# A retention block and a squared-ReLU feed-forward in one kernel: the fifth piece of w_in is converted behind chunk 4's mask, and one half step of the first layer moves ahead of chunk 4's scores

## The chip, the cores and the metric

The kernel runs on one core of a Trainium2 chip. The metric is the time of one execution on the device in microseconds; the median of several executions is given. The trace of one further execution shows what each engine did and when.

## The reference

Two blocks follow one another. The first is retention without a softmax: with `rel[i,j] = i - j`, every head has its own decay, and the masked, decayed scores are multiplied by `v`. The second is a feed-forward with a squared ReLU. q, k, v are float32; the two weights come as float64 and are rounded to float32 inside the kernel.

```python
# retention: batch 8, heads 8, seq 576, head_dim 64
scores = scale * np.matmul(q, k.transpose(0, 1, 3, 2))
gamma = 1.0 - 2.0 ** (-5.0 - np.arange(H, dtype=np.float32))
Dmat = np.where(rel >= 0, gamma[:, None, None] ** rel[None, :, :], 0.0)
attn = np.matmul(scores * Dmat[None], v)
# bridge: (B,H,S,D) -> (B*S, H*D), 4608 tokens x 512
x = np.ascontiguousarray(attn.transpose(0, 2, 1, 3)).reshape(B * S, H * D)
# feed-forward: w_in 512 x 2048, w_out 2048 x 512
h = np.maximum(x @ w_in, 0.0)
out = h * h @ w_out
```

## The kernel before

Retention goes over 40 chunks of up to 128 tokens (five per sequence: four of 128 and one of 64; chunk 4 is the short one). 512 tokens (chunks 0 to 3) make a block of the feed-forward. Everything that this change touches happens in the first tenth of the run, where retention, the first block of the first layer, and the conversion of w_in from float64 are woven together by the order in which the program issues them. Engines run on their own, but each one takes its instructions in the order issued.

**Conversion.** w_in is cut into 16 pieces. A piece is fetched raw (`fetch_w`, 512 KB) and rounded by six steps: five for VectorE (DVE), and one, `beside`, of two instructions for ScalarE (ACT). The generator `w_in_parts` yields the steps; `convert(n)` issues the next n. Pieces 0 to 3 take 6 steps each; piece 4 takes 8, as the first two of piece 5 come inside it; after that every piece j is `beside j, one j+1, two j+1, three j, four j, last j`.

```python
def round_parts(j):
    ...
    def one():      # exponent bits
        nc.vector.tensor_scalar(exp, hi, 20, 0x7FF, op0=ALU.logical_shift_right, op1=ALU.bitwise_and)
    def two():
        nc.vector.tensor_scalar(bits, as_dst(j, hi), 0xFFFFF, 0x100000, op0=ALU.bitwise_and, op1=ALU.bitwise_or)
    def beside():
        nc.scalar.activation(exp, exp, AF.Relu, bias=exp_bias[:, 0:1], scale=2.0 ** 23)
        nc.scalar.activation(frac, lo, AF.Copy, scale=2.0 ** -52)
    def three():
        nc.vector.scalar_tensor_tensor(t, bits, 2.0 ** -20, as_dst(j, frac), op0=ALU.mult, op1=ALU.add)
    def four():
        nc.vector.tensor_tensor(t, t, as_dst(j, exp_of(j)), op=ALU.mult)
    def five():
        nc.vector.scalar_tensor_tensor(bits, as_dst(j, hi), 0x80000000, bits, op0=ALU.bitwise_and, op1=ALU.bitwise_or)

def w_in_parts():
    parts = [round_parts(j) for j in range(N_W1)] + [[None] * 2]
    for j in range(N_W1):                       # N_W1 = 16
        one, two, beside, three, four, five = parts[j]
        if j <= N_ALONE:                        # N_ALONE = 4
            yield from (one, two)
        yield beside
        if j >= N_ALONE:
            yield from parts[j + 1][0:2]
        yield three
        yield four
        def last(five=five):
            five()
            n_made[0] += 1
            if n_next[0]:
                fetch_raw(2)
        yield last
```

**A step of the first block.** `first_in(j)` multiplies piece j with the block's tokens; `first_in(j, (0,))` and `(1,)` do only one half of the tokens. `step()` takes the next from the list: second halves of pieces 0, 1, 2, then pieces 3 to 15 whole.

```python
def first_in(j, halves=(0, 1)):
    assert n_made[0] > j
    ...
    p = ps_f.tile([128, 2, HT], F32, tag="f", name="h_ps")
    for c in range(N_DM):
        nc.tensor.matmul(p..., lhsT=w[:, c, :], rhs=xT[0][:, c, lo * HT:hi * HT], ...)
    nc.scalar.activation(t, p, AF.Relu)
    some(2)                                     # what is queued, the squares of steps before among it
    queue.append(lambda: nc.vector.tensor_tensor(t, t, t, op=ALU.mult))
    ...
```

**A chunk.** `turn(i)` transposes k and q (TensorE, PE), ACT copies kT, DVE makes qT (times the decay from chunk 4 on); `scores(i)` multiplies them and DVE masks the result. From chunk 4 on, the transposes and the scores take turns in one PSUM buffer. `retain_a/b/c(i)` make chunk i's output; `retain_b` ends with a small ACT copy (u_sb from x_ps), and `retain_c` writes more into x_ps.

```python
def turn(i):
    p = ps_t.tile([128, 2, 512], F32, tag="t", name="t_ps")...      # bufs=1
    ... nc.tensor.transpose(...)
    nc.scalar.copy(to, p[...])                                      # kT
    nc.vector.tensor_tensor(to, p[...], dq[...], op=ALU.mult)       # qT, i >= N_EARLY
def scores(i):
    both = ps_t.tile([128, 2, 512], F32, tag="t", name="sc_ps")...  # i >= N_EARLY
    ... nc.tensor.matmul(sc..., lhsT=kT..., rhs=qT...)
    nc.vector.tensor_tensor(r[:cs], both[:cs], msk..., op=ALU.mult) # ret
    nc.gpsimd.tensor_tensor(vs[:cs], ...)
```

**The order in the main loop** (N_EARLY = 4):

```python
for i in range(N_CH + 1):
    if i <= N_EARLY:
        if i == 1: convert(2)
        elif i == 2: convert(5)
        if i >= 1:
            retain_a(i - 1)
            if i < 3: warm(4, False)
            elif i == N_EARLY: turn(i)
            else:
                convert(1); first_in(1, (0,)); convert(5)
            retain_b(i - 1)
            ...
            retain_c(i - 1)
        convert((0, 1, 1, 0, 0)[i])
        scores(i)
        if i == 2:
            convert(5); first_in(0, (0,))
        elif i == 3:
            convert(1); first_in(2, (0,)); convert(5)
        elif i == N_EARLY:
            fetch_raw(2)
            convert(1)
            for _ in range(2):
                step(); convert(5); convert(1)
        if i < N_EARLY: ... turn(i + 1)
    else:
        retain_a(i - 1)
        if i < N_CH: turn(i)
        ffn(i - 1, 0)          # first block: convert(6), step()
        retain_b(i - 1)
        if i < N_CH: scores(i)
        retain_c(i - 1)
        ffn(i - 1, 1)          # first block: step(), convert(6), step(), convert(6)
    if i == 0: fetch_raw(2)
    if i + 3 < N_CH: load(i + 3)
    if 0 < i < N_EARLY: fetch_raw(1)
```

After the first block the first layer runs on with seven products in place of eight (Strassen-Winograd, `ffn_in`), and then the second layer (`inner`, `outer`); neither is touched.

Of the kernel before, what the change touches and what calls it, by code (L numbers as in the profile page):

```python
# [40 lines left out]
def kernel(  # L41
# [87 lines left out]
    N_EARLY = TOK // C  # L129
# [65 lines left out]
    def fetch_w(j):  # L195
        if j < len(pieces) and wide:
            nc.sync.dma_start(raw_of(j).bitcast(I64).rearrange("p (c f) -> p c f", c=N_DM), piece_src(j))
# [38 lines left out]
    def sum_w_in(mp):  # L236

        a11, a12, a21, a22, s1, s2, s4 = (w_in[mp][:, :, j, :, :].rearrange("p m c f -> p m (c f)") for j in range(NP))
        return [lambda: nc.vector.tensor_tensor(s1, a21, a22, op=ALU.add),
                lambda: nc.vector.tensor_tensor(s2, s1, a11, op=ALU.subtract),  # L240
                lambda: nc.vector.tensor_tensor(s4, a12, s2, op=ALU.subtract),
                lambda: nc.vector.tensor_tensor(a21, a11, a21, op=ALU.subtract)]
# [43 lines left out]
    def fetch_raw(count):  # L286

        for _ in range(count):
            if n_raw[0] < min(N_W1, n_made[0] + N_RAW):
                fetch_w(n_raw[0])  # L290
                n_raw[0] += 1
# [25 lines left out]
    def convert(count):  # L317
        for _ in range(count):
            f = next(w_in_steps, None)
            f and f()  # L320
# [39 lines left out]
    def rows(half, n=64):  # L360
        return slice(64 * half, 64 * half + n)
# [13 lines left out]
    def scale_q(i, engine):  # L375

        ci, t = chunks[i][1], loaded[i][0]
        engine.tensor_tensor(t, t, dv[:, :, NCH + ci:NCH + ci + 1].to_broadcast([C, H, D]), op=ALU.mult)
# [22 lines left out]
    def scores(i):  # L401

        b_, ci, c0, cs = chunks[i]
        qT, kT = st[i]["qT"], st[i]["kT"]
        if i < N_EARLY:

            sc = [ps_f.tile([128, 512], F32, tag="f", name="sc_ps")[:, 0:256].rearrange("p (h t) -> p h t", h=HP) for e in range(2)]
        else:
            both = ps_t.tile([128, 2, 512], F32, tag="t", name="sc_ps")[:, :, 0:256].rearrange("p e (h t) -> p e h t", h=HP)
            sc = [both[:, e, :, :] for e in range(2)]  # L410
        n_h = cs // CH
        for hp in range(HP):
            for h in range(n_h):
                for e in range(2):
                    t = slice(CH * h, CH * h + CH)
                    nc.tensor.matmul(sc[e][rows(h), hp, :], lhsT=kT[rows(e), hp, t], rhs=qT[rows(e), hp, t],  # L416
                                     start=True, stop=True, skip_group_check=True)
        r = st[i]["ret"] = work2.tile([128, 2, HP, CH], F32, tag="ret", name="ret")
        if i < N_EARLY:
            for e in range(2):  # L420
                nc.vector.tensor_tensor(r[:cs, e, :, :], sc[e][:cs], msk[:cs, 0, :, :].to_broadcast([cs, HP, CH]), op=ALU.mult)
        else:
            nc.vector.tensor_tensor(r[:cs], both[:cs], msk[:cs].to_broadcast([cs, 2, HP, CH]), op=ALU.mult)
        vs = st[i]["vs"] = loaded[i][2]
        nc.gpsimd.tensor_tensor(vs[:cs], vs[:cs],  # L425
                                dv[:cs, :, ci:ci + 1].to_broadcast([cs, H, D]), op=ALU.mult)
# [21 lines left out]
    def retain_a(i):  # L448

        b_, ci, c0, cs = chunks[i]  # L450
        xp[0] = ps_x.tile([128, 2, 256], F32, tag="x", name="x_ps", padded_shape=[128, 2, 512])
        clean.clear()
        if ci == 0:
            u_ps[0] = ps_u.tile([128, HP, D], F32, tag="u", name="u_ps")
        if cs < C:
            return
        own, grow = within(i, 1)
        for j in range(0, len(own), 2):
            for f in own[j:j + 2] + grow[j:j + 2]:
                f()  # L460
        grown(i, 0)
# [51 lines left out]
    def sum_x(n):  # L513

        x = xT[n]
        b11, b12 = x[:, 0:2, 0:HT], x[:, 0:2, HT:]
        b21, b22 = x[:, 2:4, 0:HT], x[:, 2:4, HT:]
        t1, t2, t4 = (xs_room[:, j, :, :] for j in range(3))
        xs[n] = {"B11": b11, "T3": b12, "B21": b21, "B22": b22, "T1": t1, "T2": t2, "T4": t4}
        return [lambda: nc.vector.tensor_tensor(t1, b12, b11, op=ALU.subtract),  # L520
                lambda: nc.vector.tensor_tensor(t2, b22, t1, op=ALU.subtract),  # L521
                lambda: nc.vector.tensor_tensor(b12, b22, b12, op=ALU.subtract),
                lambda: nc.vector.tensor_tensor(t4, b21, t2, op=ALU.subtract)]
# [21 lines left out]
    def some(count=1):  # L545
        for f in queue[:count]:
            f and f()
        del queue[:count]

    def first_in(j, halves=(0, 1)):  # L550

        assert n_made[0] > j
        wi, m, e = pieces[j]
        mp, mm = divmod(m, 2)
        p = ps_f.tile([128, 2, HT], F32, tag="f", name="h_ps")
        w = w_in[mp][:, mm, 2 * e:2 * e + 2, :, :].rearrange("p s c f -> p (s c) f")
        lo, hi = halves[0], halves[-1] + 1
        p = p[:, lo:hi, :]
        for c in range(N_DM):
            nc.tensor.matmul(p.rearrange("p h t -> p (h t)"), lhsT=w[:, c, :], rhs=xT[0][:, c, lo * HT:hi * HT],  # L560
                             start=(c == 0), stop=(c == N_DM - 1))

        t = g_room[mp % 2][:, 3:7:3, mm, :] if e else g_room[mp % 2][:, 0:5:4, mm, :]
        t = t[:, lo:hi, :]
        nc.scalar.activation(t, p, AF.Relu)

        some(2)
        queue.append(lambda: nc.vector.tensor_tensor(t, t, t, op=ALU.mult))
        if mm and e and hi == 2:
            queue.append(lambda: [nc.sync.dma_start(  # L570
                g_dram[0, a:b, :, 2 * mp:2 * mp + 2, :].rearrange("s p m t -> p s (m t)"),
                g_room[mp % 2][:, a:b, :, :].rearrange("p s m t -> p s (m t)")) for a, b in QUARTERS])
        if j >= N_W1 - 4:

            sums_w.setdefault(0, sum_w_in(0)).pop(0)()
            if n_next[0] > 1:
                if 1 not in sums_x:
                    sums_x[1] = sum_x(1)
                sums_x[1].pop(0)()
# [80 lines left out]
    def step():  # L660
        n, f, *args = steps.pop(0)
        done[0] += 1
        f(*args)
# [54 lines left out]
    for i in range(N_CH + 1):  # L718
        if i <= N_EARLY:

            if i == 1:
                convert(2)
            elif i == 2:
                convert(5)
            if i >= 1:
                retain_a(i - 1)
                if i < 3:
                    warm(4, False)
                elif i == N_EARLY:
                    turn(i)  # L730
                else:
                    convert(1)
                    first_in(1, (0,))
                    convert(5)
                retain_b(i - 1)
                if i < 3:
                    warm(4, False)
                retain_c(i - 1)
            convert((0, 1, 1, 0, 0)[i])
            scores(i)  # L740
            if i == 2:
                convert(5)
                first_in(0, (0,))
            elif i == 3:
                convert(1)
                first_in(2, (0,))
                convert(5)
            elif i == N_EARLY:
                fetch_raw(2)
                convert(1)  # L750
                for _ in range(2):
                    step()
                    convert(5)
                    convert(1)
            if i < N_EARLY:
                if i + 1 < N_EARLY:
                    scale_q(i + 1, nc.gpsimd)
                if i < 2:
                    warm(6, False)
                if i + 1 < N_EARLY:  # L760
                    turn(i + 1)
        else:
            if i == N_EARLY + 1:
                gone[0] = TOK
            retain_a(i - 1)
            if i < N_CH:
                turn(i)
            ffn(i - 1, 0)
            retain_b(i - 1)
            if i < N_CH:  # L770
                scores(i)
            retain_c(i - 1)
            ffn(i - 1, 1)
        if i == 0:
            fetch_raw(2)
        if i + 3 < N_CH:
            load(i + 3)
        if 0 < i < N_EARLY:
            fetch_raw(1)
# [239 lines left out]
```

## Time and profile before

| what | value |
|---|---|
| time, median of 3 (lowest to highest) | 999.09 us (998.42 to 999.68) |
| span of the profiled execution | 996.4 us |
| PE, busy | 975.9 us, 98% of the span |
| DVE, busy | 747.7 us, 75% |
| ACT, busy | 190.7 us, 19% |
| GpSimd (POOL), busy | 83.9 us, 8% |

The profile's second part cuts the span into 40 slices of 24.9 us and gives each engine's busy share in tenths, and PEclk, the clock granted to PE in tenths of the full one:

```
PE   7789999999999999999999999999999999999998
DVE  4687497657878797897886777877777677777765
PEclk9889999999999999999999999999999999999999
DMA  9993565754786879779558999674674757556351
```

Apart from the last slice, only the first three have PE below nine tenths. That is where chunks 0 to 5 and the start of the first block lie.

In the DMA row, 9 means that the 16 DMA engines were at work nearly all of the slice.

### The profile page before, as it was taken

How to read it: one execution, taken by the hardware profiler on the slowest of the kernel's cores; microseconds unless marked ns; L12 is line 12 of the kernel's file. 1: busy time of each engine (PE TensorE's matmuls, PEld its weight loads, DVE VectorE, ACT ScalarE, POOL GpSimd, SP SyncE). 2: the span in 40 equal slices, each digit the busy share in tenths (PEclk: the TensorE clock that was granted, in tenths of full speed). 3: DMA queues.
4: the chain of work that ended last, by engine and by line, in shares of the span. 5: the costliest groups of instructions: out<-in, count | busy, mean ns of one | idle time of the engine just before them, and what ended most of it. 6: DMA issues, size and time to landing. Idle time of an engine off the chain costs nothing.

```text
span 996.4 us, 24418 instructions
## 1 busy us (share of the span) xinstructions
PE 975.9 (98%) x10524; PEld 869.9 (87%) x10524; DVE 747.7 (75%) x1426; ACT 190.7 (19%) x461; POOL 83.9 (8%) x85
## 2 busy tenths in 40 slices
PE   7789999999999999999999999999999999999998
PEld 7645688888888888888888889999999999999998
DVE  4687497657878797897886777877777677777765
ACT  3444231112222322312221000000000000000000
POOL 3101021011111111111011000000000000000000
PEclk9889999999999999999999999999999999999999
DMA  9993565754786879779558999674674757556351
GB/s 204 249 252 115 155 190 173 184 183 135 239 278 198 233 217 289 208 202 293 149 191 298 398 391 343 245 282 170 244 249 153 275 191 274 180 224 215 124 212 44
DMA packets 187676, 220.40 MB, mean 221 GB/s; under 512 B 119216, under 2 KB 137648, under 8 KB 178608
## 3 DMA queue, kind: packets, MB, share of 16 engines
q1 hardware_dynamic: 185456, 218.31, 67.3%
q8 instruction: 83, 1.36, 0.6%
q10 hardware_dynamic: 2112, 0.52, 0.2%
q14 instruction: 25, 0.20, 0.1%
HBM read 129.41 MB, written 89.39 MB: 220 GB/s over the span
## 4 chain that ended last, share of the span: by engine, by line
PE 92%; DVE 4%; ACT 1%; DMA 1%; issue 1%; SPq 1%; DVEq 0%; ACTq 0%
PE o_b L870 17%; PE h_b L596 16%; PE o_c L870 11%; PE o_a L870 11%; PE h_c L596 11%; PE h_a L596 11%; PE h_ps L560 5%; PE x_ps L437 3%; PE t_ps L388 2%; PE x_ps L472 2%; PE sc_ps L416 2%; PE u_ps L440 1%; DMA w<-in_moe_w_in_dram 1%; PE idle_ps L712 0%; DVE room L603 0%
## 5 line engine op out<-in xcount | busy, mean ns | idle before, releaser
L596 PE MATMUL h_b<-room,w 128*128 128x256 f32 x736 | 177.2, 383 | 1.6 <-DVE room L521 0.9
L596 PEld LDWEIGHTS h_b<-room,w 128*128 128x128 f32 x736 | 137.2, 190 | 21.9 <-PE t_ps L388 1.1
L870 PE MATMUL o_b<-w,room 128*128 128x128 f32 x1168 | 144.5, 275 | 0.2 <-DVE room L821 0.2
L870 PEld LDWEIGHTS o_b<-w,room 128*128 128x128 f32 x1168 | 137.2, 192 | 0.5 <-DVE room L821 0.4
L870 PE MATMUL o_c<-w,room 128*128 128x128 f32 x1008 | 123.0, 275 | 0.0
L870 PEld LDWEIGHTS o_c<-w,room 128*128 128x128 f32 x1008 | 117.7, 192 | 0.0
L596 PE MATMUL h_c<-room,w 128*128 128x256 f32 x480 | 114.3, 381 | 0.0
L596 PE MATMUL h_a<-room,w 128*128 128x256 f32 x448 | 107.5, 383 | 0.0
L596 PEld LDWEIGHTS h_c<-room,w 128*128 128x128 f32 x480 | 90.5, 190 | 12.5
L596 PEld LDWEIGHTS h_a<-room,w 128*128 128x128 f32 x448 | 83.8, 190 | 11.8
L870 PE MATMUL o_a<-w,a 128*128 128x128 f32 x688 | 85.6, 275 | 0.0
L870 PEld LDWEIGHTS o_a<-w,a 128*128 128x128 f32 x688 | 81.2, 192 | 0.1
L613 POOL TENSOR_TENSOR room<-room 128x512 f32<-128x512 f32 x32 | 36.2, 1132 | 435.9 <-ACT room L612 380.5
L603 DVE SCALAR_TENSOR_TENSOR room<-room 128x512 f32<-128x512 f32 x96 | 67.6, 705 | 3.3
L884 ACT COPY r<-o_a 128x128 f32<-128x128 f32 x53 | 14.2, 267 | 271.4 <-PE o_a L870 235.8
L560 PE MATMUL h_ps<-room,w 128*128 128x512 f32 (+1 forms) x152 | 62.1, 560 | 1.2 <-DVE w L229 1.0
L437 PEld LDWEIGHTS x_ps<-ret,v_ld 64*64 64x64 f32 x1152 | 40.6, 138 | 15.5 <-issue 12.9
L615 DVE TENSOR_TENSOR room<-h_b,room 128x512 f32<-128x512 f32 x32 | 22.1, 691 | 42.0 <-PE h_b L596 42.0
L437 PE MATMUL x_ps<-ret,v_ld 64*64 64x64 f32 x1152 | 50.1, 227 | 2.9 <-ACT u_sb L475 2.8
L560 PEld LDWEIGHTS h_ps<-room,w 128*128 128x128 f32 x152 | 29.7, 203 | 25.4 <-issue 21.5
L425 POOL TENSOR_TENSOR v_ld<-v_ld,dv 128x512 f32<-128x512 f32 (+1 forms) x40 | 44.2, 1108 | 69.2 <-DMA v_ld<-in_v_dram 47.6
L880 DVE TENSOR_TENSOR small<-o_b,small 128x128 f32<-128x128 f32 x62 | 18.1, 292 | 38.3 <-PE o_b L870 38.3
(109 smaller groups left out, 1378.1 us busy)
## 6 DMA issues: line engine op xcount, KB each, us to landing
g_dram<-room SPq DMA_DIRECT2D x32, 1792.0 KB, 7.9
a<-g_dram SPq DMA_DIRECT2D x43, 1024.0 KB, 7.2
room<-g_dram SPq DMA_DIRECT2D x20, 1024.0 KB, 6.5
w<-w_dram SPq DMA_DIRECT2D x7, 1792.0 KB, 12.0
out_dram<-room SPq DMA_DIRECT2D x17, 512.0 KB, 3.4
w<-in_moe_w_in_dram SPq DMA_DIRECT2D x16, 512.0 KB, 5.9
w<-in_moe_w_out_dram SPq DMA_DIRECT2D x16, 512.0 KB, 3.7
v_ld<-in_v_dram SPq DMA_DIRECT2D x31, 256.0 KB, 4.3
```

The source lines that it names most:

```text
L388: nc.tensor.transpose(p[:, h, j, hp, :], loaded[i][j][rows(h), 2 * hp:2 * hp + 2, :], ident[rows(h), rows(h)])
L416: nc.tensor.matmul(sc[e][rows(h), hp, :], lhsT=kT[rows(e), hp, t], rhs=qT[rows(e), hp, t], start=True, stop=True, skip_group_check=True)
L425: nc.gpsimd.tensor_tensor(vs[:cs], vs[:cs], dv[:cs, :, ci:ci + 1].to_broadcast([cs, H, D]), op=ALU.mult)
L437: own.append(lambda hp=hp, e=e, b=b: nc.tensor.matmul(x_at(hp, b, h), lhsT=s["vs"][rows(h), 2 * hp + b, :], rhs=s["ret"][rows(h), e, hp, : ...
L472: nc.tensor.matmul(x_at(hp, b, h), lhsT=u[rows(e), hp, :], rhs=s["qT"][rows(e), hp, CH * h:CH * h + CH], start=clears(b, hp // 2), stop=Fa ...
L560: nc.tensor.matmul(p.rearrange("p h t -> p (h t)"), lhsT=w[:, c, :], rhs=xT[0][:, c, lo * HT:hi * HT], start=(c == 0), stop=(c == N_DM - 1))
L596: nc.tensor.matmul(p[:, mm, :], lhsT=w[:, c, :], rhs=xs[n][right][:, c, :], start=(j in OPENS and mm == 0 and c == 0), stop=(j in CLOSES a ...
L603: nc.vector.scalar_tensor_tensor(t, t, 0.0, t, op0=ALU.max, op1=ALU.mult)
L613: nc.gpsimd.tensor_tensor(g["A11"], g["A11"], g["A11"], op=ALU.mult)
L615: nc.vector.tensor_tensor(g["A22"], p, p15, op=ALU.add)
L870: nc.tensor.matmul(p, lhsT=s["lefts"][left][:, m, :], rhs=w_out[j][:, m, WO_SLOT[right], :], start=(i in OPENS and m == 0), stop=(i in CLO ...
L880: nc.vector.tensor_tensor(s["u2"], p, s["p1"], op=ALU.add)
```

## The change

At chunk 3, three conversion steps are issued behind the step `first_in(2, (0,))` and not five: steps one and two of piece 4 no longer stand between piece 3's last step and chunk 4's qT. At chunk 4, the raw fetch and a first `step()` (second half of the tokens with piece 0) come before the scores, between chunk 3's products and chunk 4's scores; after the scores (whose last part is the mask on DVE) come one, two and beside of piece 4, the second `step()`, and five steps more. In all, chunk 4's visit issues 8 conversion steps, not 13; with the two fewer at chunk 3, the conversion stands seven steps earlier when chunk 5 begins: at the end of piece 4, and no longer at `beside` of piece 6. From there on the same calls of `convert(6)` take it on, so that each of them begins with `beside` of a piece in place of ending with it.

What it is for: chunk 4's qT no longer waits in DVE's queue for the raw data of piece 4, PE has a product to do meanwhile, and chunk 5's qT comes earlier in DVE's queue.

```diff
@@ main loop, i <= N_EARLY @@
             convert((0, 1, 1, 0, 0)[i])
+            if i == N_EARLY:
+                fetch_raw(2)
+                step()
             scores(i)
             if i == 2:
                 convert(5)
                 first_in(0, (0,))
             elif i == 3:
                 convert(1)
                 first_in(2, (0,))
-                convert(5)
+                convert(3)
             elif i == N_EARLY:
-                fetch_raw(2)
-                convert(1)
-                for _ in range(2):
-                    step()
-                    convert(5)
-                    convert(1)
+                convert(3)
+                step()
+                convert(5)
```

No instruction is added or taken away on PE, DVE, ACT or GpSimd; only their order changes. On the queue that issues the DMAs, the loads of chunk 7 now stand ahead of the fetches of pieces 10 and 11.

More of the change, by code (lines that the diff above doesn't have):

```diff
@@ L746 @@
                 first_in(2, (0,))
+                convert(3)
+            elif i == N_EARLY:
+                convert(3)
+                step()
                 convert(5)
-            elif i == N_EARLY:
-                fetch_raw(2)
-                convert(1)
-                for _ in range(2):
-                    step()
-                    convert(5)
-                    convert(1)
             if i < N_EARLY:
```

## The prediction

> **What bounds the kernel now.** I read the page first, then the waits of PE in stretches, then the timelines of DVE, ACT and PE from 20 to 70 us, and last the granted clock by the microsecond. PE is busy 98% of the span, and its waits (engine, what it waited for, us in total, times, longest) lie almost all at the start. From 25 to 60 us:
>
> ```profile
> PE sc_ps L416 <- DVE qT L398: 5.7, 2, 3.1
> DVE w L211 <- DMA w<-in_moe_w_in_dram: 6.5, 2, 3.4
> PE x_ps L437 <- ACT u_sb L475: 1.5, 3, 0.9
> ```
>
> Behind that, from 120 to 400 us, one wait is listed for PE:
>
> ```profile
> PE h_b L596 <- DVE room L521: 0.9, 1, 0.9
> ```
>
> So what is won before about 60 us should reach the end nearly one to one, and nothing else can be won. DVE's timeline (start, duration, and in brackets idle before and its releaser) shows why the two scores wait:
>
> ```profile
> 34.50 0.69 DVE L229 SCALAR_TENSOR_TENSOR w<-w,w 128x512 uint32<-128x512 uint32 x1
> 38.26 0.43 DVE L211 TENSOR_SCALAR w<-w 128x512 uint32<-128x512 uint32 x1 [3.07 <-DMA w<-in_moe_w_in_dram]
> 38.94 0.42 DVE L398 TENSOR_TENSOR qT<-t_ps,dq 128x256 f32<-128x256 f32 x1
> 45.02 0.43 DVE L211 TENSOR_SCALAR w<-w 128x512 uint32<-128x512 uint32 x1 [3.42 <-DMA w<-in_moe_w_in_dram]
> 47.14 0.69 DVE L229 SCALAR_TENSOR_TENSOR w<-w,w 128x512 uint32<-128x512 uint32 x1
> 48.08 0.42 DVE L211 TENSOR_SCALAR w<-w 128x512 uint32<-128x512 uint32 x1
> 50.21 0.69 DVE L229 SCALAR_TENSOR_TENSOR w<-w,w 128x512 uint32<-128x512 uint32 x1
> 50.81 0.68 DVE L398 TENSOR_TENSOR qT<-t_ps,dq 128x512 f32<-128x512 f32 x1
> ```
>
> 38.26 is step one of piece 4, waiting for its raw data; qT of chunk 4 stands behind it, though its kT copy was done at 35.12. 45.02 is step one of piece 5, waiting again; behind it come the rest of piece 4, all of piece 5, and only then qT of chunk 5. PE's timeline has the other side:
>
> ```profile
> 39.41 1.12 PE L416 MATMUL sc_ps<-qT,kT 64*64 64x64 f32 x16 [3.10 <-DVE qT L398]
> 51.55 1.13 PE L416 MATMUL sc_ps<-qT,kT 64*64 64x64 f32 x32 [2.59 <-DVE qT L398]
> 53.60 1.12 PE L437 MATMUL x_ps<-ret,v_ld 64*64 64x64 f32 x16 [0.92 <-ACT u_sb L475]
> 54.65 8.70 PE L560 MATMUL h_ps<-room,w 128*128 128x512 f32 x16
> ```
>
> The last line is pieces 3 and 4, ending at 63.35; the same pair takes 7.13 us at 69.62, at full clock. Table by microsecond (PE busy, count, granted clock, DMA share, GB/s):
>
> ```profile
> 36.00:37.00 1.00, 0.31 (x24) 1.00 1.07 288
> 39.00:40.00 1.00, 0.59 (x11) 0.50 0.56 123
> 45.00:46.00 1.00, 1.00 (x7) 1.00 1.09 367
> 52.00:53.00 1.00, 0.68 (x28) 0.50 0.77 159
> 56.00:57.00 1.00, 1.00 (x2) 0.50 1.26 212
> 58.00:59.00 1.00, 1.00 (x4) 1.00 1.06 265
> ```
>
> In quarter-microsecond steps the clock is 0.50 from 37.4 to 44.1 and from 51.0 to 57.8.
>
> [...]
>
> **The change part by part.**
> Chunk 4's qT: DVE ends piece 3 at about 35.15 and goes straight on to qT, done at 35.6 and not 39.36. PE ends chunk 3's products at 36.31; ACT's copy of the block's last tokens runs 36.35 to 36.94. The moved half step takes 1.97 us (from 31.48), so 36.99 to 38.96; then the scores at full clock, half of the 0.65 us of 32 (30.29), to 39.3; the second half step to 41.3; the transposes of chunk 5 (0.65) to 42.0; the half step of piece 2 to 44.0; chunk 4's 16 products with u to 44.4. The idle of 3.1 us has shrunk to 0.7, and with it the half clock of the first stretch should go. But none of this is the gain by itself, for PE then waits again.
>
> Chunk 5's qT: piece 5's data still lands at 45.0, because its fetch is issued at 39.20 in both kernels, behind the loads of chunk 6, which are issued back to back. DVE does one and two of 5, then three, four and last of 4, as before, to about 47.8. Then comes qT at once. What leaves the way is one and two of 6 and three, four, last of 5: 48.08 to 50.81 is 2.73, with the square at 47.75 (0.33) 3.06 us. So qT runs 47.75 to 48.4, and the scores start at about 48.5 and not 51.55: 3.1 us.
>
> Chunk 4's products (L437): before, they waited 0.92 us behind ACT, whose small copy stood behind beside of piece 7. In the new order of ACT it stands behind beside of piece 5 and one half step, done by 47.2. The 0.92 us go: 4.0 us in all.
>
> Clock: the wait on PE from 44.4 to 48.5 is 4.1 us, so the clock falls again. At full clock the work from the scores to the end of piece 4 is 0.6 + 0.55 + 7.13 = 8.3 us, to 56.8. Half clock held for 6.25 us after the restart at 51.55 before. The restart is now without a gap, [...] I take 2.3. End of piece 4: 59.1 in place of 63.35, a gain of 4.3.
>
> After that PE is full. Each convert(6) now begins with beside j, which stands on ACT behind the ReLU of the step before it. With T for the end of piece 4's product: its ReLU starts at T, beside takes till T + 1.8 (63.35 to 65.15 before), three, four and last of piece 7 to T + 3.85, qT of chunk 6 to T + 4.55. PE needs it at T + 5.1 (68.46 less 63.35). It fits by half a microsecond, in chunks 6, 7 and 8 alike. A DVE instruction now and then takes 0.7 us longer (1.43 at 75.99), so I take off 0.2 for that. Sum: 3.1 + 0.9 + 0.3 - 0.2 = 4.1 us; 999.1 - 4.1 = 995.0.
>
> **The rivals.**
> (a) The wait only moves. Chunk 4's scores come 3 us earlier and PE stands longer before chunk 5's. This is true of the first part, which is why I count nothing for it; it would be the whole story if qT of chunk 5 kept its place, and the new order says it does not. Then 998 to 999.
> (b) The new order of ACT and DVE becomes the bound: beside behind the ReLU, DVE waiting in three, qT late. Against it are the 0.5 us of slack; for it, that the slack is smaller than one of DVE's slow instructions. At 0.5 us lost in each of three chunks the time is 996.5.
> (c) The clock. [...] the half-clock stretch is short or missing, 993.3; if the long stretch stays, or the first one also remains, 996.
> (d) Piece 5 lands later or earlier. Everything in DVE hangs on that landing; the load of chunk 7 is now issued at some 44 us and not 51.4, when pieces 6 to 9 are under way. A microsecond later makes a microsecond of time.
> (e) Piece 10's and 11's fetches stand behind chunk 7's loads; their first steps come some 10 us after, so I expect no wait.
>
> **Range and chances.** The median before spreads by 1.3 us over 3 runs. (c) and (d) are worth about 1.5 us each way, (b) up to 1.5 up. Predicted 995.0, range 993.0 to 997.2. 2% is 20 us, five times the most that these waits hold, so within 2% it is almost surely: 0.985; faster 0.007, slower 0.008.
>
> **What would show each step right or wrong.** In the profile of the changed kernel: DVE's L398 of 128x256 at about 35.2 with no DMA wait ahead of it; PE's half step at 37.0 ahead of the scores; L211 still waiting for its DMA until 45; L398 of 128x512 at about 47.8; PE's only long wait the one before the scores at 48.5, and none for the small ACT copy; half clock only around 48 to 54; the end of piece 4 at 59. It is wrong if chunk 6 to 8's scores wait for qT, if the gain at 60 us is gone at 115, or if piece 5 lands elsewhere.

## The result, and the profile after

| | before | changed |
|---|---|---|
| time, median (lowest to highest), 4 runs each | 998.83 us (998.42 to 999.68) | 993.42 us (992.08 to 994.71) |
| ratio, 95% interval | | 0.9945 (0.9927 to 0.9962) |
| span of the profiled execution | 996.4 us | 990.9 us |

The change is worth 5.4 us, about half a per cent. Measured again later, in five runs beside the experiments, the changed kernel took 995.05 us against 999.34, ratio 0.9957 (0.9945 to 0.9969): 4.3 us. The two intervals overlap.

The waits of PE in the changed kernel from 25 to 130 us (engine, line, waited for, us in total, times, longest):

```profile
PE sc_ps L416 <- DVE qT L398: 2.3, 1, 2.3
PE h_ps L560 <- DVE w L229: 0.9, 2, 0.6
PE h_ps L560 <- ACT room L494: 0.7, 1, 0.7
PE x_ps L437 <- ACT u_sb L475: 0.6, 2, 0.3
```

The scores wait once and not twice, 2.3 us and not 5.7. ACT's small copy costs 0.6 us where it cost 1.5: the 0.92 us ahead of chunk 4's products is gone. New is 0.7 us for the block's last tokens, ahead of the moved half step. DVE's timeline shows the new order:

```profile
36.17 0.42 DVE L398 TENSOR_TENSOR qT<-t_ps,dq 128x256 f32<-128x256 f32 x1
40.66 0.68 DVE L423 TENSOR_TENSOR ret<-sc_ps,msk 64x512 f32<-64x512 f32 x1 [3.73 <-PE sc_ps L416]
41.27 0.41 DVE L211 TENSOR_SCALAR w<-w 128x512 uint32<-128x512 uint32 x1
44.34 0.43 DVE L211 TENSOR_SCALAR w<-w 128x512 uint32<-128x512 uint32 x1 [1.99 <-DMA w<-in_moe_w_in_dram]
46.46 0.69 DVE L229 SCALAR_TENSOR_TENSOR w<-w,w 128x512 uint32<-128x512 uint32 x1
47.07 0.68 DVE L398 TENSOR_TENSOR qT<-t_ps,dq 128x512 f32<-128x512 f32 x1
56.04 0.69 DVE L223 SCALAR_TENSOR_TENSOR w<-w,w 128x512 f32<-128x512 uint32 x1 [3.62 <-ACT w L220]
```

Chunk 4's qT no longer has a DMA wait ahead of it, step one of piece 4 stands behind the mask, and chunk 5's qT follows the last step of piece 4. Piece 5 is still waited for, until 44.34. The last line is new: step three of piece 6 waits 3.6 us, because its beside now stands on ACT behind the ReLU of piece 3. PE's timeline:

```profile
38.01 1.99 PE L560 MATMUL h_ps<-room,w 128*128 128x256 f32 x8 [0.68 <-ACT room L494]
39.93 0.68 PE L416 MATMUL sc_ps<-qT,kT 64*64 64x64 f32 x16
45.04 0.46 PE L472 MATMUL x_ps<-qT,u_sb 64*64 64x64 f32 x16
47.81 0.80 PE L416 MATMUL sc_ps<-qT,kT 64*64 64x64 f32 x32 [2.31 <-DVE qT L398]
48.37 1.08 PE L437 MATMUL x_ps<-ret,v_ld 64*64 64x64 f32 x16
49.38 8.25 PE L560 MATMUL h_ps<-room,w 128*128 128x512 f32 x16
62.46 0.46 PE L472 MATMUL x_ps<-qT,u_sb 64*64 64x64 f32 x16
62.92 0.69 PE L416 MATMUL sc_ps<-qT,kT 64*64 64x64 f32 x32
```

The pair of pieces 3 and 4 ends at 57.63 (49.38 + 8.25), 5.72 us ahead of 63.35. Last, the table by microsecond (width of the stretch, PE busy, count, granted clock, DMA share, GB/s):

```profile
45.00:46.00 1.00, 0.50 (x17) 1.00 1.03 346
48.00:49.00 1.00, 1.00 (x44) 0.63 1.09 365
50.00:51.00 1.00, 1.00 (x2) 0.50 1.20 252
52.00:53.00 1.00, 1.00 (x4) 1.00 0.55 114
```

Full clock now holds from 30 us up to 48.3 us, just behind the wait before chunk 5's scores, and the half clock that follows lasts 3.4 us and not 6.8.

### The profile page after: what moved, and what is told of

The parts are those of the page before. It is cut to its first block, busy times and chain, and to the rows that moved or that the text cites. A ratio compares the mean times of both kernels' runs of the same rounds, so it can differ in the third digit from the quotient of the medians.

```text
span 990.9 us, 24417 instructions
## 1 busy us (share of the span) xinstructions
PE 973.1 (98%) x10524; PEld 868.6 (88%) x10524; DVE 746.9 (75%) x1426; ACT 189.9 (19%) x461; POOL 83.9 (8%) x85
## 4 chain that ended last, share of the span: by engine, by line
PE 93%; DVE 4%; SPq 1%; DMA 1%; issue 1%; ACT 1%; DVEq 0%; ACTq 0%
PE o_b L870 17%; PE h_b L596 17%; PE o_c L870 11%; PE o_a L870 11%; PE h_c L596 11%; PE h_a L596 11%; PE h_ps L560 5%; PE x_ps L437 3%; PE t_ps L388 2%; PE x_ps L472 2%; PE sc_ps L416 2%; PE u_ps L440 1%; DMA w<-in_moe_w_in_dram 1%; PE idle_ps L712 0%; SPq L150 0%
## 5 line engine op out<-in xcount | busy, mean ns | idle before, releaser
L560 PE MATMUL h_ps<-room,w 128*128 128x512 f32 (+1 forms) x152 | 60.1, 543 | 1.6 <-DVE w L229 0.9
L425 POOL TENSOR_TENSOR v_ld<-v_ld,dv 128x512 f32<-128x512 f32 (+1 forms) x40 | 44.3, 1110 | 64.1 <-DMA v_ld<-in_v_dram 53.9
```

Of the source, the lines that this page charges most:

```text
L425: nc.gpsimd.tensor_tensor(vs[:cs], vs[:cs], dv[:cs, :, ci:ci + 1].to_broadcast([cs, H, D]), op=ALU.mult)
```

## The experiments

My theory was: the gain is that chunk 5's qT stands ahead of piece 5's conversion; the first wait, at chunk 4's scores, is worth nothing by itself; and whatever PE gains up to the end of the pair reaches the end. The rivals were that the first wait and its half clock were the gain, and that the conversion on DVE is the real bound. Each kernel was timed in five rounds, and the kernel before was timed again in each group.

**The front part alone (e1).** The changed kernel with the seven steps issued at chunk 4 again:

```diff
             elif i == N_EARLY:
                 convert(3)
                 step()
-                convert(5)
+                convert(12)
```

> The changed kernel, but the seven conversion steps that it takes from chunk 4's visit are issued there again (convert(12) for convert(5)). Chunk 4's qT and the moved half step stay as changed; only chunk 5's qT goes back behind piece 5. My theory (the gain is chunk 5's qT, the first wait is worth nothing by itself): chunk 4's scores start at about 39 to 40 us without a wait for qT, PE then idles 6 to 7 us before chunk 5's scores at about 51, the pair of pieces 3 and 4 ends at about 63, and the time is that of the kernel before, 998 to 999.5. The rival (the first wait and its half clock are what was gained): 993 to 995.5.

Measured: 998.78 us against 999.23, ratio 0.9997 (0.9989 to 1.0005). No gain at all. Its PE timeline:

```profile
40.70 0.68 PE L416 MATMUL sc_ps<-qT,kT 64*64 64x64 f32 x16
51.79 1.13 PE L416 MATMUL sc_ps<-qT,kT 64*64 64x64 f32 x32 [5.52 <-DVE qT L398]
54.89 9.73 PE L560 MATMUL h_ps<-room,w 128*128 128x512 f32 x16
```

The first wait is gone, and the second has grown to 5.52 us, about as much as both together before (5.7). The rival of the first wait falls.

**The other part alone (e2).** The kernel before with its conversion at chunk 4 ended at piece 4:

```diff
             elif i == N_EARLY:
                 fetch_raw(2)
                 convert(1)
-                for _ in range(2):
-                    step()
-                    convert(5)
-                    convert(1)
+                step()
+                convert(5)
+                step()
```

> The kernel before, with only the conversion in chunk 4's visit ended seven steps earlier, at the end of piece 4; steps one and two of piece 4 still stand ahead of chunk 4's qT, and the half step still comes after the scores. My theory: chunk 4's scores still wait about 3 us for qT and PE falls to half clock at about 38 us, but chunk 5's qT comes straight behind piece 4, at about 47 to 48, PE arrives at chunk 5's scores at about 48.5 to 49 with no wait left and at full clock, the pair of pieces 3 and 4 ends at about 57.5, and the time is that of the changed kernel, 992.5 to 994.5. The rival (the half step ahead of the scores and the early qT of chunk 4 make the gain, or both parts are needed): 996 to 999.

Measured: 993.91 us against 999.23, ratio 0.9945 (0.9933 to 0.9958), the full gain of the change. Its PE timeline:

```profile
40.10 0.68 PE L416 MATMUL sc_ps<-qT,kT 64*64 64x64 f32 x16 [3.08 <-DVE qT L398]
48.90 0.65 PE L416 MATMUL sc_ps<-qT,kT 64*64 64x64 f32 x32
50.06 7.13 PE L560 MATMUL h_ps<-room,w 128*128 128x512 f32 x16
```

Here the first wait stays and the second is gone: PE comes late enough to chunk 5's scores to find qT there, and at full clock (32 products of the scores in 0.65 us, the pair in 7.13). So fewer steps at chunk 4 are the gain, and the other edits of the change, among them the one that its name puts first, add nothing that shows within these intervals (about 1.3 us each way).

**The half step put back behind the scores (e5).**

```diff
             if i == N_EARLY:
                 fetch_raw(2)
-                step()
             scores(i)
...
             elif i == N_EARLY:
+                step()
                 convert(3)
                 step()
                 convert(5)
```

> The changed kernel with the half step put back behind chunk 4's scores; the conversion steps stay as changed. My theory: chunk 4's scores start at about 36.5 us in place of 40, the half step at about 37.5, and from there all is as in the changed kernel, since chunk 5's qT hangs on piece 5's landing: 992.5 to 994.5. The rival (the half step between is what keeps the clock and the order of ACT, and is part of the gain): 1 us or more slower than the changed kernel, 995 or more.

Measured: 994.87 us against 999.23, ratio 0.9955 (0.9941 to 0.9969), outside the 992.5 to 994.5 of my theory but the same ratio as the second measurement of the changed kernel (0.9957). The time lies between the ranges of my theory and of its rival, so a loss of up to about 1 us from the half step's place is not excluded. Chunk 4's scores ran at 35.92, and PE then waited 5.96 us before chunk 5's.

**The changed kernel again (e0)**, beside the next three:

> The changed kernel as it is, on the chip of the three that follow: 992.5 to 994.7, as measured before. In its trace chunk 5's scores again wait about 2 to 4 us for qT[...].

Measured: 995.05 us (993.26 to 996.57), a little over what was expected. The profile of this run had piece 5 landing later than the first one:

```profile
46.25 0.43 DVE L211 TENSOR_SCALAR w<-w 128x512 uint32<-128x512 uint32 x1 [4.34 <-DMA w<-in_moe_w_in_dram]
48.98 0.68 DVE L398 TENSOR_TENSOR qT<-t_ps,dq 128x512 f32<-128x512 f32 x1
```

Step one of piece 5 came 1.91 us later than in the first profile, qT 1.91 us later, and the span was 993.2 and not 990.9. PE waited 4.67 us before chunk 5's scores, more than the 2 to 4 expected.

**Piece 5 fetched ahead of chunk 6's loads (e6).**

```diff
+        if i == N_EARLY - 1:
+            fetch_raw(1)
         if i + 3 < N_CH:
             load(i + 3)
-        if 0 < i < N_EARLY:
+        if 0 < i < N_EARLY - 1:
             fetch_raw(1)
```

> The changed kernel with piece 5 fetched ahead of chunk 6's loads and not behind them. Theory (chunk 5's qT hangs on piece 5's landing): the data lands about 6 us earlier, at about 39, step one of piece 5 no longer waits for a DMA, qT of chunk 5 is at about 45, PE's wait before chunk 5's scores all but goes, full clock stays, the pair of pieces 3 and 4 ends at about 54 and the time is 989.5 to 991. The rival (the landing does not matter, the sum of DVE's conversion work sets chunk 5's qT): within 0.5 us of the changed kernel. Another (the loads of chunk 6 are then late): a new wait on DMA for chunk 6's transposes.

Measured: 988.35 us (987.82 to 988.97) against 999.34, ratio 0.9891 (0.9878 to 0.9903). That is 11.0 us under the kernel before, twice what the change brings or more, and better than the 989.5 expected at best. DVE's timeline:

```profile
40.97 0.41 DVE L211 TENSOR_SCALAR w<-w 128x512 uint32<-128x512 uint32 x1
43.82 0.68 DVE L398 TENSOR_TENSOR qT<-t_ps,dq 128x512 f32<-128x512 f32 x1
46.95 0.43 DVE L211 TENSOR_SCALAR w<-w 128x512 uint32<-128x512 uint32 x1 [2.44 <-DMA w<-in_moe_w_in_dram]
```

Step one of piece 5 (40.97) waits for nothing, qT runs at 43.82, and the wait for raw data has moved to piece 6, behind qT, where PE doesn't feel it. The pair ended at 52.77, after the 7.13 us that it takes at full clock. Both rivals fall: DVE has the same conversion work, and from 40 to 130 us no wait of PE on a DMA is listed.

**The same edit in the kernel before (e9)**, to see whether the earlier data alone would have done:

> The kernel before with one edit: piece 5 fetched ahead of chunk 6's loads, as in e6. It asks whether the earlier data alone would have done. Theory (chunk 5's qT stands behind the whole of piece 5 and the first steps of piece 6, so another landing takes its place): step one of piece 5 no longer waits, but step one of piece 6, which still stands ahead of qT, now waits for its own data until about 47; qT comes at about 49.5 to 50, 1 us earlier, and the time is 997 to 998.8. The rival (the landing of piece 5 is the whole matter, the order is not): 992 to 995.

Measured: 997.13 us against 998.98, ratio 0.9976 (0.9968 to 0.9985). Between a third and a half of the change's gain, as expected, since piece 6 takes piece 5's place ahead of qT:

```profile
41.98 0.41 DVE L211 TENSOR_SCALAR w<-w 128x512 uint32<-128x512 uint32 x1
47.55 0.43 DVE L211 TENSOR_SCALAR w<-w 128x512 uint32<-128x512 uint32 x1 [2.41 <-DMA w<-in_moe_w_in_dram]
50.29 0.68 DVE L398 TENSOR_TENSOR qT<-t_ps,dq 128x512 f32<-128x512 f32 x1
```

**Chunk 5's qT ahead of piece 5 (e4).** No conversion step after the second half step at chunk 4; the later calls stay:

```diff
             elif i == N_EARLY:
                 convert(3)
                 step()
-                convert(5)
```

> The changed kernel without the last five conversion steps of chunk 4's visit (no convert(5) there), so that chunk 5's qT stands ahead of piece 5's first step and its wait for the data. The later calls of convert(6) stay, so beside of a piece ends each call again. My theory: qT of chunk 5 runs at about 44, the wait of 2.3 us before chunk 5's scores is gone, PE stays at full clock, the pair of pieces 3 and 4 ends at about 54 and the time is 989 to 990.5. The rival (DVE has no room left, the conversion then becomes the bound and PE waits for piece 4, 5 or 6 instead): a new wait of PE for a piece's last step, and 992.5 to 995.

Measured: 992.72 us against 999.23, ratio 0.9936 (0.9923 to 0.9948): less than I expected. The scores ran at 45.50 without a wait and the clock stayed full (the pair took 7.13 us, the mean granted clock was 1.0), but another wait took the place:

```profile
45.50 0.65 PE L416 MATMUL sc_ps<-qT,kT 64*64 64x64 f32 x32
47.84 0.68 PE L437 MATMUL x_ps<-ret,v_ld 64*64 64x64 f32 x16 [1.69 <-ACT u_sb L475]
48.45 7.13 PE L560 MATMUL h_ps<-room,w 128*128 128x512 f32 x16
```

ACT's small copy stood behind beside of piece 5, which waits for piece 5's data. It is the wait of 0.92 us of the kernel before, in a larger size. The time lies in the rival's range, but the rival's sign, a wait of PE for a piece's last step, is not in the profile. That profile is of the fastest of the five runs (990.40; the others took 992.51 to 993.79), so it shows this kernel at its best.

**That beside issued later (e8).** On top of the last edit, at chunk 5's visit:

```diff
+            if half and i == N_EARLY:
+                convert(1)
-            for f in (step, lambda: convert(6)) if half else (lambda: convert(6), step):
+            for f in (step, lambda: convert(6)) if half else (lambda: convert(5 if i == N_EARLY else 6), step):
                 f()
```

> e4 (chunk 5's qT ahead of piece 5), with beside of piece 5 issued behind chunk 4's products and not ahead of them, so that ACT's small copy no longer stands behind it. e4 showed 1.69 us of wait for that copy. Theory (that wait is on the path, as 0.92 us of it was in the kernel before): it goes, the pair of pieces 3 and 4 ends at about 54 in place of 55.6, and the time is 990.5 to 991.5. The rival (PE then waits for piece 4's last step instead): a wait of PE for the last step of a piece, and 992 or more.

Measured: 989.32 us (988.64 to 989.49) against 999.34, ratio 0.9901 (0.9886 to 0.9915). The copy's wait is gone, the pair ends at 53.90. The 3.4 us between these two medians are more than the wait of 1.69 us; the two profiles, each of its kernel's fastest run, differ by 1.8 us. e4's wait hangs on piece 5's landing, which spreads from run to run, and that may be the rest; it is not shown.

**Both cures together (e10)**, this and the earlier fetch:

> e8 and e6 together: chunk 5's qT ahead of piece 5, beside of piece 5 later, and piece 5 fetched ahead of chunk 6's loads. Each alone took PE's wait before chunk 5's scores away. Theory (both cure the same wait, so they do not add): 987.5 to 989.5, no more than 0.8 us under the better of the two. The rival (they take away different waits): 985 to 987.

Measured: 988.21 us (987.69 to 988.62) against 998.98, ratio 0.9891 (0.9877 to 0.9906). They cure the same wait and do not add.

**The clock (e7).** Idle products ahead of chunk 5's scores, in the changed kernel:

```diff
+            if i == N_EARLY + 1:
+                warm(9, True)
             if i < N_CH:
                 scores(i)
```

> The changed kernel with nine idle products (128x128, results unused) on PE ahead of chunk 5's scores, to fill the wait there; they take about 2.2 us. Theory [...]: full clock through, the pair of pieces 3 and 4 takes 7.1 and not 8.3 us or more, time 991.5 to 992.5, that is 1 to 2 us under the changed kernel. The rival (the clock is not what costs, the gap itself is): no difference.

Measured: 992.95 us (991.64 to 997.19) against 999.34, ratio 0.9943 (0.9927 to 0.9959), 2.1 us under the changed kernel in the same group, but the intervals overlap. Its profile is of the slowest of the six runs (997.19; the others took 991.64 to 994.61): there piece 5 landed so late that 2.56 us of wait were left behind the idle products, and the clock fell all the same (pair 9.38 us, mean granted clock 0.995). The other five runs have mean clocks of 0.995 to 1.0, the fastest 1.0. Not conclusive.

**All profiles in one table.** The end of the pair is the start of its line plus the duration; the rest is the span less that end, to within 0.1 us.

| kernel | step one of piece 5 | pair took | pair ends | rest of the span |
|---|---|---|---|---|
| before | 45.02 | 8.70 | 63.35 | 933.1 |
| front part alone | 45.59 | 9.73 | 64.62 | 933.0 |
| before, early fetch | 41.98 | 8.83 | 62.52 | 933.4 |
| with idle products | 47.41 | 9.38 | 62.17 | 933.3 |
| half step behind | 45.85 | 8.83 | 60.06 | 933.1 |
| changed, second profile | 46.25 | 8.31 | 59.93 | 933.3 |
| changed | 44.34 | 8.25 | 57.63 | 933.3 |
| fewer steps alone | 44.59 | 7.13 | 57.19 | 933.3 |
| qT ahead of piece 5 | 45.64 | 7.13 | 55.58 | 933.1 |
| and beside later | 44.73 | 7.13 | 53.90 | 933.0 |
| both cures | 44.39 | 7.13 | 53.55 | 933.1 |
| changed, early fetch | 40.97 | 7.13 | 52.77 | 933.3 |

Behind the pair, all twelve take 933.0 to 933.4 us. Whatever the front wins, arrives.

Differences of a microsecond in the pair's end can be chance. Chunk 4's transposes start between 33.70 and 35.79 us in these profiles, in part because PE stood 0.5 to 2.4 us at about 20 us for a reason that the profiles don't show. Where PE waits for piece 5 later, this is swallowed; where it doesn't, it goes straight into the end. The last three rows take 18.60, 18.59 and 19.06 us from chunk 4's transposes to the pair's end, so the order among them is that of their first 35 us, and the earlier fetch takes nothing more away once chunk 5's qT stands ahead of piece 5.

## Why the prediction was right

995.0 was predicted with a range of 993.0 to 997.2; 993.42 was measured. The direction, the mechanism and the chance of a change within 2% were right, and the gain was larger than the 4.1 us of the sum. By its steps:

- **The first part counts nothing.** Shown: without the second part it is worth nothing (ratio 0.9997), and without the first part the second brings all (0.9945).
- **Chunk 5's qT, 3.1 us.** The scores started at 47.81, 3.74 us earlier. The surplus of 0.68 is the landing of piece 5, 44.34 in place of 45.02, which I had taken as fixed. It isn't: over the profiles with the old place of the fetch, step one of piece 5 came between 44.3 and 47.4. In six of them (before, changed, e1, e2, e4, e5) the fetch was issued between 39.17 and 40.87 and took 4.8 to 6.0 us to land.
- **ACT's small copy, 0.92 us.** Gone, as said; the kernel with qT ahead of piece 5 shows what it costs when it comes back.
- **The clock, 0.3 us.** This was the term most out of size. Half clock lasted 3.4 us, from 48.3 to 51.7. The 2.3 us of loss that I took for it were my estimate; no trace stood behind them. The pair took 8.25 us, 1.12 over the 7.13 of full clock; scores and products took 1.57 from 47.81 to 49.38, against 1.17 (45.60 to 46.77) in the kernel with beside later; so 1.5 us were lost and not 2.3. Before, it was 1.57 in the pair, and 1.01 in the stretch of 3.10 from 51.55 to 54.65, less 0.92 of wait and 1.17: 2.6 us. The gain is 1.1 us.
- **The new order on ACT and DVE, 0.2 us off.** Chunk 6's scores started 0.46 us after the products with u and not 0.28 (62.46 and 62.92, against 68.18 and 68.46), so nearly 0.2 us were lost there; the wait of 3.6 us of step three costs PE no more than that. The cause is the one that I had taken the 0.2 us off for: an instruction of DVE took 1.43 us and not 0.69 (L229 at 57.50), and qT of chunk 6 ended 5.2 us behind the pair and not 4.55, where PE needed it at 5.1. The rest of the span is 0.2 us longer, but such differences lie among the other kernels too.

The sum in the profiles: 3.74 + 0.92 + 1.06 = 5.72 us at the end of the pair, less 0.2, makes the 5.5 us between the two spans. Of the rivals, (a) was right for the first part alone, (b) was there without weight, and (c) and (d) made the surplus. In the profile of the second measurement piece 5 came 1.23 us later than in the kernel before and the low clock cost 0.39 us more than in the first profile (10.21 us from the scores to the end of the pair, and not 9.82), so that the pair ended only 3.42 us earlier (1.83 + 0.92 + 0.67). The median gain of its five runs is 4.3 us; that it is so close to the 4.1 predicted is partly luck, for the two terms that I could not know differ between the two profiles of this kernel: the landing by 1.91 us, the clock by 0.39.

Some smaller points were wrong. The moved half step started at 38.01 and not 37.0, since all of PE's work ahead of it ran 1.0 us later than in the kernel before; nothing came of it, as PE then waits for piece 5. The 2% are not five times what the waits listed hold: these come to 8.1 us (5.7 + 1.5 + 0.9), and 20 us is two and a half times that.

What I missed: all of this hangs on where the fetch of one piece stands in the queue that issues the DMAs. I wrote that it was behind the loads of chunk 6, took it as given, and did not ask what moving it would bring. On top of the change it brings more than the change itself, 6.7 us (988.35 against 995.05); alone, in the kernel before, it brings 1.9.

## What to carry to other kernels

When two waits of an engine follow one another, ask of the second what it hangs on before crediting the first: time won ahead of a wait that has its own cause is only longer idling there. On DVE and ACT here, an instruction that waited for a DMA, or for another that did, held up all that stood behind it (chunk 4's qT by 3.1 us, ACT's copy by 1.69), so a small operation that another engine needs should be issued ahead of it, and the fetch itself ahead of loads that are needed later. And a wait taken away may put its neighbour in its place: here a copy of 0.15 us on ACT behind a conversion step.

## What the runs showed of the hardware that I had not expected

The spread of a kernel's times seems to come from such a chain. The changed kernel's nine runs lie between 992.08 and 996.57 (the first four alone spread by 2.6 us); the three kernels in whose profile PE no longer waits for a piece's data (e6, e8, e10) spread by 0.9 to 1.2 us, in four runs each (987.82 to 988.97, 988.64 to 989.49, 987.69 to 988.62). Where such a wait is left the spread stays wide: 3.4 us in five runs of e4, 4.6 us in eighteen of e9.

The half-clock stretches, apart from the one that the run's end cuts off, lasted 6.83 us each in the kernel before (from 37.4 and from 51.0 us) and 3.41 us each in the changed one (from 20.9 and from 48.3 us). What follows a wait on PE was not the same after nearly the same wait. Before chunk 4's scores it was 3.10 us in the kernel before and 3.08 with fewer steps alone. In the first, the 16 products of the scores took 1.12 us and the two half steps behind them 5.54; in the second, 0.68, as in the changed kernel at full clock (39.93), and 5.41. From the start of the scores to chunk 5's transposes it was 6.53 us (39.41 to 45.94) and 5.95 (40.10 to 46.05). What decides this is not shown.

The time that the queue takes to issue DMAs held up a transfer here. In the changed kernel eight loads stand between the fetch of piece 4 (32.45) and that of piece 5 (39.17); they went out one by one, and 6.7 us passed:

```profile
32.45 0.61 SPq L197 DMA_DIRECT2D w<-in_moe_w_in_dram  x1
33.11 1.64 SPq L138 DMA_DIRECT2D dq<-in_decay_q_dram  x1
34.86 0.56 SPq L148 DMA_DIRECT2D q_ld<-in_q_dram  x1
35.46 1.02 SPq L150 DMA_DIRECT2D q_ld<-in_q_dram  x2
36.58 0.41 SPq L148 DMA_DIRECT2D k_ld<-in_k_dram  x1
37.03 1.58 SPq L150 DMA_DIRECT2D k_ld<-in_k_dram  x2
38.66 0.47 SPq L145 DMA_DIRECT2D v_ld<-in_v_dram  x1
39.17 4.04 SPq L197 DMA_DIRECT2D w<-in_moe_w_in_dram  x5
```

Each line is an issue on that queue, or several of one kind, with its start and duration. With the fetch of piece 5 moved up to right behind that of piece 4 (e6), the two went out together in 1.21 us:

```profile
32.56 1.21 SPq L197 DMA_DIRECT2D w<-in_moe_w_in_dram  x2
```
